# One weave delay and the writer of two constants, in a pooled-attention and mixer kernel on one core

## The chip, the core and the metric

The kernel runs on one core of one Trainium2 chip. Five engines work side by side: TensorE (PE in the profile; its weight loads are PEld), VectorE (DVE), ScalarE (ACT), GpSimd (POOL) and SyncE (SP), each with an instruction stream of its own. Transfers are issued by SyncE, GpSimd and, for one output, ScalarE. The metric is the time of one execution on the device in microseconds (us); less is better.

## What is computed

Eight batches, each with 8 heads, 576 rows and a head dimension of 64. Keys and values are averaged over groups of 8 rows, which leaves 72 of each; attention runs over these. The result, laid out as 576 x 512 per batch, goes through a mixer: one two-layer network across the rows (576 to 256 to 576) and one across the channels (512 to 1536 to 512), each with a residual.

```python
k_p = k.reshape(B, H, Sp, pool, D).mean(axis=3)
v_p = v.reshape(B, H, Sp, pool, D).mean(axis=3)
scores = scale * np.matmul(q, k_p.transpose(0, 1, 3, 2))
scores = scores - np.max(scores, axis=-1, keepdims=True)
attn = np.exp(scores)
attn = attn / (np.sum(attn, axis=-1, keepdims=True) + 1e-09)
x = np.matmul(attn, v_p)          # then laid out as (batch, 576, 512)

xt = x.transpose(0, 2, 1)
h = np.maximum(xt @ w_tok1, 0.0) @ w_tok2
u = x + h.transpose(0, 2, 1)
h2 = np.maximum(u @ w_ch1, 0.0) @ w_ch2
out = u + h2
```

## The kernel before

**Tiles.** Of a batch's 576 rows, 512 form four main blocks of 128, and 64 are a tail. The tails of two batches share one tile of 128 partitions; the groups are [0, 7], [1, 2], [3, 4], [5, 6], and a batch's slot is its place in its group. Matmul operands are bf16.

**Start.** The first batch's keys, queries and values are loaded in pieces: half of the keys as raw f32 through SyncE and cast by VectorE, the rest by GpSimd's transfers (`load_main0`, L152). Meanwhile two constant matrices are built: `pool_m` (128 x 72, L172) holds 1/8 where a row belongs to a pooled row, and `diag` (128 x 16, L180) the same for the tail, from which VectorE copies `pool_t` (L189). Each is first filled with 1/8 and then cut to a band by two affine selects on GpSimd. TensorE sums keys and values by multiplying with these matrices. `idle` is a zero tile whose matmuls keep TensorE running during the wait (L261). Instructions of this part are put in order by the framework's scheduler, per engine.

**Stages.** From `tc.manual_schedule` on, the order of the text is the order of each engine's instructions. The loop runs over b = 0 to 7. Its main stream is `c_stream(b)`, the channel network of batch b: 12 steps of hidden-layer matmuls (`do_GT`, L1007, with the ReLU L1009 on ScalarE), then for each of four row blocks three steps of output matmuls (L1023), the residual add on VectorE (L1027) and a write by SyncE (L1055). A batch in slot 1 adds the tail of its group: 3 + 3 more steps. Each step is given a cost of 864.

Beside it runs a side stream: `value_stream(b + 1)` and `score_stream(b + 2)`.

- `value_stream` begins with issues: the transpose of the next batch's queries (`qT_dma`, SyncE) and `load_gated(b + 2)` on GpSimd, which copies one element of the last transposed probabilities into `gate` (L984) and so holds back the loads behind it. Then come the steps of values: `a.do_AV` and `c.do_AV`, two of each, and `t.do_AV` for a pair of tails (cost 1150 each). One multiplies transposed probabilities `pT` with the pooled values (L468) and normalises on VectorE (L472, L473). Then `mix_stream`: the tail's part of the row network (`do_tails`, L608), the first layer for the main blocks (`do_AT`, L615, ReLU on ScalarE and VectorE), the second layer (`do_u`, L672, added on VectorE L673), and transposes of the result by SyncE's transfers (`do_uT`, L684).
- `score_stream` holds the scores (`do_S`, L390), maximum and shift on VectorE (L396, L398), the exponential on ScalarE (`do_E`, L406), and the transpose of the probabilities into `pT` by a transfer that SyncE issues (`do_PT`, L412).

**The weave.** `weave(main, side, delay, lead)` puts the two streams into one order by their costs: the main stream runs alone until `delay` of its cost is spent, and then a side item is taken whenever the side's share lies at or behind the main stream's share, with `lead` left at the end.

```python
    tm, ts = max(main.total() - delay - lead, 1e-9), max(side.total(), 1e-9)
    cm, cs = -delay, 0.0
        take_side = im >= len(main.items) or (ia < len(side.items) and cs / ts <= cm / tm)
```

A delay of 1728 is two steps of the main stream, 3456 four. The call is in the loop's last line (L1096):

```python
            weave(c_stream(b), side, 1728.0 if b == 0 else 3456.0 if b == 1 else 1728.0, 3456.0 if b == B - 2 else 1728.0)
```

Of the kernel before, what the change touches and what calls it, by code (L numbers as in the profile page):

```python
# [28 lines left out]
def weave(main, side, delay=0.0, lead=0.0):  # L29


    tm, ts = max(main.total() - delay - lead, 1e-9), max(side.total(), 1e-9)
    im = ia = 0
    cm, cs = -delay, 0.0
    while im < len(main.items) or ia < len(side.items):
        take_side = im >= len(main.items) or (ia < len(side.items) and cs / ts <= cm / tm)
        if take_side:
            c, fn = side.items[ia]
            ia += 1
            cs += c  # L40
        else:
            c, fn = main.items[im]
            im += 1
            cm += c
        fn()
# [3 lines left out]
def kernel(  # L49
# [16 lines left out]
    nc = tc.nc  # L66
    B, H, S, D = q.shape
# [4 lines left out]
    POOL = 8  # L72
# [97 lines left out]


    pool_m = singles.tile([P, SP], BF16)  # L172
    nc.gpsimd.memset(pool_m, 1.0 / POOL)
    nc.gpsimd.affine_select(out=pool_m, in_=pool_m, pattern=[[-2, SP]], compare_op=ALU.is_ge,
                            fill=0.0, base=0, channel_multiplier=1)
    nc.gpsimd.affine_select(out=pool_m, in_=pool_m, pattern=[[2, SP]], compare_op=ALU.is_ge,
# [1 line left out]

    load_main0(k, main_t[0][0], HP, H)
    diag = singles.tile([P, P // POOL], BF16)  # L180
    nc.gpsimd.memset(diag, 1.0 / POOL)
    nc.gpsimd.affine_select(out=diag, in_=diag, pattern=[[-POOL, P // POOL]], compare_op=ALU.is_ge,
                            fill=0.0, base=0, channel_multiplier=1)
    nc.gpsimd.affine_select(out=diag, in_=diag, pattern=[[POOL, P // POOL]], compare_op=ALU.is_ge,
# [747 lines left out]
    def score_stream(st, b):  # L932

        add = adder(st)
        a, c, t = parts[b]
        own = owned(b)
        add(SC, a.do_S, 0)
        add(SC, a.do_S, 1)
        add(0, a.do_E, 0)
        for bb in own[1:]:  # L940
            add(KP, pool_k, bb)
        add(SC, a.do_S, 2)
        add(0, a.do_E, 1)
        add(0, a.do_E, 2)
        add(0, a.do_PT, 0)
        add(0, a.do_PT, 1)
        if t:
            add(2 * SC, t.do_S)
        add(SC, c.do_S, 0)
        if t:  # L950
            add(0, t.do_E)
            add(0, t.do_PT)
        add(SC, c.do_S, 1)
        add(0, c.do_E, 0)
        add(SC, c.do_S, 2)
        add(0, c.do_E, 1)
        add(0, c.do_E, 2)
        add(0, c.do_PT, 0)
        add(0, c.do_PT, 1)

    def value_stream(st, b):

        add = adder(st)
        a, c, t = parts[b]
        if b + 1 < B:
            units(b + 1)
            add(0, qT_dma, b + 1)
        if b + 2 < B:
            add(0, load_gated, b + 2, lambda: c.pT[1][:, 0, 0:1])
        add(AV, a.do_AV, 0)  # L970
        add(AV, a.do_AV, 1)
        if t and len(t.bs) == 1:
            add(AV, t.do_AV)
        add(AV, c.do_AV, 0)
        if t and len(t.bs) > 1:
            add(AV, t.do_AV)
        add(AV, c.do_AV, 1)
        mix_stream(st, b, owned(b + 1)[:1] if b + 1 < B else ())
# [70 lines left out]
    def c_stream(b):  # L1049
        st = Stream()  # L1050
        g = group_of[b]

        def dst_main(j, cols, o_sb):
            q = nc.gpsimd if b == B - 2 and j == 0 else nc.sync if cols.start == 0 else nc.scalar
            q.dma_start(out=out[b, 0:MAIN, cols].rearrange("(p j) n -> p j n", j=NJ)[:, j, :], in_=o_sb)  # L1055

        def dst_tail(j, cols, o_sb):
            for s, bb in enumerate(groups[g]):
                nc.sync.dma_start(out=out[bb, MAIN:S, :], in_=o_sb[half[s], :])

        wide, chunk = channel_mix(lambda kk, t0, t1: uT_main[b][:, t0 // P:t1 // P, kk, :],
                                  lambda j: u_main[b][:, j, :], dst_main, MAIN, 0 if b else 3)
        blocks = [wide] + [chunk(j, 2 if b == B - 1 and j == NJ - 1 else 1) for j in range(NJ)]
        if slot_of[b] == 1:
            wide, chunk = channel_mix(lambda kk, t0, t1: uT_tail[g][:, kk, t0:t1], lambda j: u_tail[g], dst_tail, P)
            at = 3 if b == B - 1 else len(blocks)
            blocks[at:at] = [wide, chunk(0)]
        for block in blocks:
            st.items.extend(block)
        return st  # L1070
# [16 lines left out]
    with tc.manual_schedule(engines=engines):  # L1087
        side1 = begin()
        for b in range(B):
            side = Stream() if b else side1  # L1090
            if 0 < b < B - 1:
                value_stream(side, b + 1)
            if b + 2 < B:
                score_stream(side, b + 2)

            weave(c_stream(b), side, 1728.0 if b == 0 else 3456.0 if b == 1 else 1728.0, 3456.0 if b == B - 2 else 1728.0)  # L1096


# [28 lines left out]
```

## Time and profile before

| | |
|---|---|
| three runs | 281.32 us median, 279.86 to 281.5 |
| the profiled execution | 280.83 us, of which the span from the first to the last instruction is 279.1 |
| granted TensorE clock | 1.000 (mean) |
| TensorE busy | 268.3 us |
| VectorE, ScalarE, GpSimd busy | 165.6, 121.9, 113.4 us |
| chain that ended last, by engine | TensorE 84%, transfers 6%, VectorE 5% |
| DMA | 42.27 MB, mean 151 GB/s |

Start times are counted from the span's start. A row of the timeline gives the start, the time from the first start to the last end, the engine, the line, the operation, what it writes and reads, the shapes and how many were merged; in square brackets stands the idle time of the engine before it and what ended that. The end of a matmul is modelled: it takes in the drain, which overlaps the next matmul, so that starts are the safer thing to compare. The chain is followed back from the last instruction: at each step to what released it.

### The profile page before, as it was taken

Reading aid. Unit: us, or ns where it says so; the run is one execution under the profiler, and the core shown is the slowest. Engines: PE = TensorE matmul, PEld = TensorE weight load, DVE = VectorE, ACT = ScalarE, POOL = GpSimd, SP = SyncE. Lnnn points to the kernel's source line nnn. Section 1 sums busy time; section 2 is a strip of 40 time slices with the busy share of each in tenths; the row PEclk is TensorE's granted clock in tenths of the full one; section 3 lists DMA queues with packets and bytes.
Section 4 is the critical chain, followed back from the end, with each engine's and each line's share of the span. In section 5 each row is a group of like instructions: output and inputs, shape, how many; then the busy total and the mean of one; then the engine's idle time right before and its main releaser. Section 6 shows DMA issues by size and latency. Waiting matters only on the chain.

```text
span 279.1 us, 5476 instructions
## 1 busy us (share of the span) xinstructions
PE 268.3 (96%) x2144; PEld 145.1 (52%) x2172; DVE 165.6 (59%) x381; ACT 121.9 (44%) x225; POOL 113.4 (41%) x162
## 2 busy tenths in 40 slices
PE   6789999999999999999999999999999999999994
PEld 4565856554545444475545454475544454554462
DVE  5597677778759853684579761785479452510112
ACT  8673688235533454035534452054623550036220
POOL 8748433697538957193449264820000000000000
PEclk9999999999999999999999999999999999999999
DMA  8999999996999999959998999759266701461013
GB/s 134 176 195 205 200 205 196 190 212 140 197 153 193 222 239 153 212 151 155 173 197 144 204 199 194 162 137 162 63 84 152 180 2 39 113 100 33 38 47 105
DMA packets 98969, 42.27 MB, mean 151 GB/s; under 512 B 68800, under 2 KB 94400, under 8 KB 98944
## 3 DMA queue, kind: packets, MB, share of 16 engines
q0 software_dynamic: 35616, 17.93, 49.1%
q1 hardware_dynamic: 63184, 23.93, 42.4%
q8 instruction: 17, 0.28, 0.4%
q10 hardware_dynamic: 144, 0.07, 0.1%
q14 instruction: 8, 0.07, 0.1%
HBM read 35.85 MB, written 9.44 MB: 162 GB/s over the span
## 4 chain that ended last, share of the span: by engine, by line
PE 84%; DMA 6%; DVE 5%; issue 1%; ACT 1%; POOL 1%; DVEq 0%; POOLq 0%
PE pa L1023 31%; PE pa L1007 30%; PE pa L672 3%; DMA pT<-prob_m 3%; PE pa L390 3%; PE pa L468 3%; DMA km<-in_k_dram 2%; PE pa L597 2%; PE pa L651 1%; DVE xm L473 1%; PE pa L615 1%; PE pt L615 1%; DVE mx L396 1%; PE pa L1039 1%; PE pt L374 1%
## 5 line engine op out<-in xcount | busy, mean ns | idle before, releaser
L1023 PE MATMUL pa<-wc,GT 128*128 128x512 bf16 (+2 forms) x427 | 102.4, 373 | 1.0 <-issue 0.2
L1009 ACT ACTIVATE GT<-pa 128x512 bf16<-128x512 f32 x105 | 62.2, 597 | 64.1 <-PE pa L1007 63.8
L1007 PE MATMUL pa<-uTm,wc 128*128 128x512 bf16 x372 | 89.3, 379 | 0.0
L1007 PEld LDWEIGHTS <-wc 128*128 128x128 bf16 x564 | 44.8, 98 | 37.1 <-issue 1.6
L1023 PEld LDWEIGHTS <-GT 128*128 128x128 bf16 x444 | 40.8, 98 | 41.5 <-issue 1.2
L406 ACT ACTIVATE prob_m<-sh 128x432 bf16<-128x432 f32 (+1 forms) x48 | 24.5, 522 | 55.2 <-DVE sh L398 55.1
L1027 DVE TENSOR_TENSOR o<-pa,um 128x512 f32<-128x512 f32 (+2 forms) x33 | 22.1, 670 | 26.4 <-PE pa L1023 26.3
L357 POOL TENSOR_TENSOR s<-vs 72x512 f32<-72x512 bf16 x24 | 27.6, 1150 | 15.7 <-DMA vs<-in_v_dram 14.2
L398 DVE TENSOR_TENSOR sh<-pa,mx 128x432 f32<-128x432 f32 (+1 forms) x48 | 26.8, 558 | 4.1
L396 DVE TENSOR_REDUCE mx<-pa 128x6 f32<-128x432 f32 (+1 forms) x48 | 26.4, 550 | 4.3 <-PE pa L390 4.1
L473 DVE TENSOR_TENSOR xm<-pa,den 128x256 bf16<-128x256 f32 x56 | 23.7, 424 | 1.9
L1055 POOL DMA_DIRECT2D out_dram<-o x1 | 0.6, 620 | 49.1 <-DVE o L1027 49.1
L472 DVE RECIPROCAL den<-pa 128x4 f32<-128x4 f32 x60 | 10.6, 176 | 16.8 <-PE pa L468 16.7
L673 DVE TENSOR_TENSOR um<-pa,xm 128x512 bf16<-128x512 f32 x24 | 16.1, 687 | 5.0 <-PE pa L672 3.7
L358 POOL TENSOR_TENSOR s<-s 72x256 f32<-72x256 f32 x24 | 17.3, 722 | 1.9
L390 PE MATMUL pa<-kbd,qT 128*128 128x144 bf16 x128 | 15.2, 226 | 0.9 <-ACT qT L378 0.7
L390 PEld LDWEIGHTS <-qT 128*128 128x128 bf16 x128 | 10.6, 98 | 9.3 <-ACT qT L378 1.3
L468 PEld LDWEIGHTS <-pT 72*128 72x128 bf16 (+1 forms) x256 | 11.2, 99 | 8.1 <-DMA pT<-prob_m 1.4
L593 DVE TENSOR_SCALAR AT<-pa 128x512 bf16<-128x512 f32 x6 | 4.1, 692 | 16.9 <-PE pa L615 9.5
L672 PE MATMUL pa<-AT,w2m 128*128 128x512 bf16 x45 | 13.1, 379 | 0.0
L468 PE MATMUL pa<-vpx,pT 72*128 72x65 bf16 (+1 forms) x256 | 12.6, 194 | 0.5 <-DMA pT<-prob_m 0.4
L1007 PE MATMUL pa<-uTt,wc 128*128 128x128 bf16 x192 | 11.9, 219 | 0.0
(151 smaller groups left out, 273.5 us busy)
## 6 DMA issues: line engine op xcount, KB each, us to landing
out_dram<-o SPq DMA_DIRECT2D x30, 256.0 KB, 2.6
vs<-in_v_dram POOLq DMA_DIRECT2D x7, 512.0 KB, 10.7
km<-in_k_dram POOLq DMA_DIRECT2D x7, 512.0 KB, 9.6
qm<-in_q_dram POOLq DMA_DIRECT2D x7, 512.0 KB, 12.8
wc<-in_moe_w_ch_dram POOLq DMA_DIRECT2D x6, 512.0 KB, 11.7
out_dram<-o SPq DMA_DIRECT2D x8, 128.0 KB, 2.4
o<-in_k_dram SPq DMA_DIRECT2D x2, 256.0 KB, 3.0
kt<-in_k_dram POOLq DMA_DIRECT2D x8, 64.0 KB, 8.0
```

The lines of the kernel that those rows point to most:

```text
L357: nc.gpsimd.tensor_tensor(out=s4, in0=vs[:, hs, 0:4], in1=vs[:, hs, 4:8], op=add)
L390: nc.tensor.matmul(out=sc[:, (h - h0) * 2:(h - h0) * 2 + 2, :], lhsT=qTs[self.b][:, 2 * h + self.jj, :], rhs=kbd[self.b % NB][:, h], start ...
L396: nc.vector.tensor_reduce(out=mx[:, 0:n], in_=sc, axis=AX.X, op=ALU.max)
L398: nc.vector.tensor_tensor(out=sh[:, 0:n], in0=sc, in1=mx[:, 0:n, None].broadcast_to([P, n, SP]), op=ALU.subtract)
L406: nc.scalar.activation(out=self.probs[:, :, h0:h1, 0:SP].rearrange("p e h n -> p h e n"), in_=self.sh[i][:, 0:(h1 - h0) * 2].rearrange("p ...
L468: nc.tensor.matmul(out=ao[r, hh, :], lhsT=probs_of(h, r), rhs=vpx[b % NB][:, h, :], start=True, stop=True)
L473: nc.vector.tensor_tensor(out=xo[rows, hf * HP * D:(hf + 1) * HP * D].rearrange("p (h d) -> p h d", d=D), in0=ao[rows, :, 0:D], in1=den[ro ...
L672: nc.tensor.matmul(out=u_ps, lhsT=w2m[:, m, j, :], rhs=ATs[b][:, m, :], start=(m == 0), stop=(m == 1))
L1007: nc.tensor.matmul(out=g_ps[:, i, :], lhsT=wc1[:, kk, m * P:(m + 1) * P], rhs=uTs(kk, 0, width), start=(kk == 0), stop=(kk == 3))
L1009: nc.scalar.activation(out=GT[:, m0:m0 + per, :], in_=g_ps, func=AF.Relu)
L1023: nc.tensor.matmul(out=hold["ps"], lhsT=GT[:, kk, j * P:(j + 1) * P], rhs=wc2[:, kk, cols], start=(kk == 0), stop=(kk == NM - 1))
L1027: nc.vector.tensor_tensor(out=o_sb, in0=hold["ps"], in1=us(j)[:, cols], op=ALU.add)
```

## The change

In the weave of b == 2 the main stream runs four steps alone and not two, before the side stream (the values of batch 3, which is the fourth batch, and the scores of batch 4) sets in; the lead at the end stays. And the fills of `pool_m` and `diag` with 1/8 are issued on VectorE and not on GpSimd; the affine selects that follow remain on GpSimd.

```diff
     pool_m = singles.tile([P, SP], BF16)
-    nc.gpsimd.memset(pool_m, 1.0 / POOL)
+    nc.vector.memset(pool_m, 1.0 / POOL)
     nc.gpsimd.affine_select(out=pool_m, in_=pool_m, pattern=[[-2, SP]], compare_op=ALU.is_ge,
                             fill=0.0, base=0, channel_multiplier=1)
...
     diag = singles.tile([P, P // POOL], BF16)
-    nc.gpsimd.memset(diag, 1.0 / POOL)
+    nc.vector.memset(diag, 1.0 / POOL)
...
-            weave(c_stream(b), side, 1728.0 if b == 0 else 3456.0 if b == 1 else 1728.0, 3456.0 if b == B - 2 else 1728.0)
+            weave(c_stream(b), side, 1728.0 if b == 0 else 3456.0 if b <= 2 else 1728.0, 3456.0 if b == B - 2 else 1728.0)
```

## The prediction, made before the change was run

> **What bounds the kernel now.** I read the page's busy times first, then the windows of 10 us, then the chain of waits with TensorE's timeline around the stage that the change touches, and at last the start.
>
> ```profile
> PE 268.3 (96%) x2144; PEld 145.1 (52%) x2172; DVE 165.6 (59%) x381; ACT 121.9 (44%) x225; POOL 113.4 (41%) x162
> ```
>
> Three lines of the windows follow (stretch, its length, busy us of PE, weight loads, DVE, ACT, POOL, then the granted clock, DMA share, GB/s):
>
> ```profile
> 0.00:10.00 10.00, 6.95 (x71) 4.74 (x72) 4.70 (x18) 7.74 (x17) 8.78 (x22) 1.00 0.99 146
> ...
> 30.00:40.00 10.00, 10.00 (x92) 7.03 (x91) 7.47 (x15) 7.86 (x16) 3.09 (x5) 1.00 1.35 202
> ...
> 90.00:100.00 10.00, 9.59 (x64) 4.75 (x64) 8.02 (x19) 5.05 (x10) 8.78 (x12) 1.00 1.23 221
> ```
>
> TensorE (PE) is the bound. From 30 us to the end most windows show it idle for 0.05 of 10 us; the worst is 90 to 100, with 0.41. Little is to be won after the start: what moves TensorE's stream by x moves the end by x, unless a later wait takes it.
>
> The changed delay acts on the third batch's channel stage (b == 2), which begins at 94.94 us. Here is TensorE there, and below it the stage of b == 4, which has the same make (a second slot, a delay of 1728, the values of a batch that opens a group, the scores of one that closes it):
>
> ```profile
> 94.94 1.89 PE L1007 MATMUL pa<-uTm,wc 128*128 128x512 bf16 x8
> 97.19 0.43 PE L468 MATMUL pa<-vpx,pT 72*128 72x65 bf16 x8 [0.36 <-DMA pT<-prob_m]
> 99.19 0.42 PE L468 MATMUL pa<-vpx,pT 72*128 72x65 bf16 x8
> 101.44 0.43 PE L468 MATMUL pa<-vpx,pT 72*128 72x65 bf16 x8
> ...
> 156.80 1.89 PE L1007 MATMUL pa<-uTm,wc 128*128 128x512 bf16 x8
> 158.53 0.42 PE L468 MATMUL pa<-vpx,pT 72*128 72x65 bf16 x8
> 160.51 0.42 PE L468 MATMUL pa<-vpx,pT 72*128 72x65 bf16 x8
> 162.50 0.42 PE L468 MATMUL pa<-vpx,pT 72*128 72x65 bf16 x8
> ```
>
> In both, two blocks of hidden-layer matmuls (L1007) run, then a step of values (L468), then two blocks, and so on. Undisturbed, the steps stand at +1.73, +3.71 and +5.70 us from the stage's start; with b == 2 at +2.25, +4.25 and +6.50. So the first step is late by 0.52 (2.25 - 1.73) and the third by a further 0.27 (6.50 - 4.25 = 2.25, against 1.99). Only 0.36 of it is listed as idle, because the drain that is modelled at a matmul's end covers the rest. The whole stage agrees: 94.94 to 128.37 is 33.43 us, 156.80 to 189.42 is 32.62; the difference is 0.81. The chain of waits names what both steps waited for:
>
> ```profile
> 91.01 6.13 DMA pT<-prob_m
> 97.19 0.43 PE pa L468 x8
> 97.63 0.56 PE pa L1007 x3
> 98.18 3.21 DMA pT<-prob_m
> 101.44 0.43 PE pa L468 x8
> ```
>
> These are transposes of probabilities by DMA, issued by SyncE. The first lands 6.13 us after its issue, the others from 98 us on in 3.2 to 3.3.
>
> **The change part by part.** *The delay.* I worked the weave through by its costs (main 25920, side 17198). Before, the side begins after two blocks of 864, now after four; `lead` is as it was, so it ends at the same place. The first step of values moves from 94.94 + 1.73 (where it can't start) to 94.94 + 3.45 = 98.39, as the stage of b == 1 shows it with the same delay (x16 of L1007 in 3.45 us). Its transpose has landed at 97.15. The second follows at 98.39 + 1.99 = 100.38; its transpose was there before 99.19. The third comes at 102.37; its transpose landed at 101.39. The last two move by as much, and their transposes are in by 102.78. So both waits go: 0.52 + 0.27 = 0.79 us, with 0.80 as the mean of this and the 0.81 of the whole stage.
>
> What is late next? The side is denser (20736 of main work for it and not 22464), and some steps change neighbours. Between the second token matmuls (AT1) and their first reader (u0) one block is left and not two: the ReLU on VectorE takes 0.69 us and starts 0.04 after TensorE's end, so the operand is there after about 0.75, and the matmul that reads it comes after 0.86 + 0.22 = 1.08. Hidden, with 0.3 to spare; if VectorE were still at the output add before it (0.69, one block earlier, so just done) the price is 0.1 to 0.3. The first token matmuls come 2.5 us after the last step of values begins (step 0.27, two blocks, four tail matmuls 0.5), and its rows were ready after 1.5 us (104.79 to 106.30). The stage of b == 1, which packs 21640 of side work into 15552, loses about 0.4 us in 20 with that, and this one packs 17198 into 20736: I take 0, between 0 and 0.3.
>
> SyncE's queue: the transpose of q of batch 4 is issued with the side's first step, but stands behind the same issues as before. Then the first `uT` transpose comes after the second output write (one issue of 0.33 us) and not before it; the next stage reads it 8 us later. GpSimd's queue: the gate copy, the loads of batch 5 and their sums keep their order, and the gate still opens when the fourth transpose lands (102.78).
>
> The scores of batch 4 fall one block later within the stage, except at its end. Their first transpose is issued at 123.95 now, right after the last output write. With TensorE 0.8 earlier, VectorE's row of shifts (0.61, 0.46 each) and adds (0.69) puts that write's add at 122.25 to 122.94, and so the transpose at about 123.4. It took 4.7 us there, so it lands near 128.1; its reader comes at 130.09 - 0.80 = 129.29. 1.2 us to spare: cost 0.
>
> *The two constants.* GpSimd loses memsets of 0.177 and 0.102 us. VectorE gains two. A 128x36 memset takes 0.088 there and a 64x256 one 0.27; 72 elements stand near 0.12, 16 near 0.07, together 0.19. They lie before VectorE's wait for the raw keys (idle 0.77 before 3.63), so they cost nothing; without that cover, 0.19. The warm-up matmuls wait for a VectorE memset there: late by up to 0.19, they push the first half of the keys' sums from 8.19, but the second half waits for the keys until 9.54, with TensorE idle 0.87 before it.
>
> New is a wait of the first mask (affine select) on GpSimd for VectorE; behind it are queued the key load and all further loads. VectorE is done by about 2.4, before GpSimd has issued the load ahead (2.97).
>
> ```profile
> 2.18 0.79 POOL L153 DMA_DIRECT2D qm<-in_q_dram  x1
> 2.97 0.18 POOL L173 MEMSET pool_m<- 128x72 bf16 x1
> 3.06 0.75 POOL L153 DMA_DIRECT2D km<-in_k_dram  x1
> 3.89 0.27 POOL L174 TENSOR_SCALAR_AFFINE_SELECT pool_m<-pool_m 128x72 bf16<-128x72 bf16 x1
> ```
>
> The key load that the start waits for (it lands at 9.5) is issued right behind the memset. Without it the issue can come 0.09 to 0.18 earlier; but the order here is a scheduler's, not the text's, and a mask that needs no memset on its own engine may now be put ahead of it: both masks (0.27 + 0.24) less the memset make it 0.33 later. Bounds: -0.18 and +0.33. I take 0, because the load ahead landed 5.3 us after its issue and this one after 6.4: 1.1 us of it are queueing, and an issue that moves by less changes only the time in the queue.
>
> The GPSIMD Engine Reference of the Trainium skill (section 4.1) says to use VectorE for elementwise work, GpSimd being at best near line rate for one input. By that alone the 0.28 us would count as a gain and the sum would be 279.75; the queueing above speaks against it.
>
> Sum: 280.83 us for the profiled execution (span 279.1, 1.73 around it) less 0.80 is 280.03. The three runs have a median of 281.32 and scatter from 279.86 to 281.5; the mean of these and the profiled one is 280.88, and 0.80 less is **280.1**, which I forecast.
>
> **The rivals.** *The wait moves one batch on* (slower than before). In the stage of b == 3 the first step of values reads the first transpose of batch 4. If that is issued a block later than now (124.81, because its shift is), and lands as slowly as the 6.13 of batch 3, it is there at 130.94, against 129.29: 1.65 lost, 0.80 won, 281.7. It decides against the change from a landing after 130.09 on. For it: the 4.7 now, so it is not a quiet place. Against it: the write ahead of it in SyncE's queue comes earlier, not later. The slow one fell among heavy traffic (221 to 250 GB/s at 90 to 97 us); at 121 to 124 us the rows show 87 GB/s, and batch 5's values had landed at 118.18. DMA: Bandwidth & Descriptors of the Trainium skill (Queues, rings and completion order) says that a DMA engine takes turns between queues packet by packet, so loads in flight would stretch a transpose; no row shows the turns themselves. 8%.
>
> *A later wait takes the gain.* Loads gated by time alone don't come earlier: 280.9. Against it: the keys of batch 6 are paired at 143.27 and read at 147.42, the values of batch 5 summed at 128.35 and read at 158.53, so 4 us and more are left. 14%.
>
> *The start moves.* The queueing doesn't cover the key load's issue: 279.8 to 280.4. 10%.
>
> *Only the listed idle is a real wait:* 0.36 won, 280.5. Against it is the 0.81 of the twin stage. 8%.
>
> **How the numbers follow.** My forecast has 54%, the four rivals 40%, and 6% are for what no row shows, above all an order at the start that holds up other loads. The range takes the forecast with 0.9 below it for scatter (half of the 1.64 of the three runs) and reaches up to the slower rival: 279.2 to 281.7. A measurement of this kernel tells about 1% (2.8 us) from no change. Faster than 278.1 would need more than all of TensorE's idle time between 30 and 270 us (2.0 us, summed over the windows): 2%. Slower than 283.7 comes from the unnamed 6% and the tail of the slower rival: 6%. The rest, 92%, lies between.
>
> **What would show it.** The changed profile should show L1007 x16 in one piece before the first L468 of the stage, no idle before it, steps of values 1.99 apart, a stage of 32.6 us, and less of "DMA pT" in the chain (3.3% now; two pieces of it gone). The key load at the start should land at 9.4 to 9.6 wherever its issue stands. I am wrong if L468 of the stage of b == 3 shows a wait for pT, if the stage stays above 33 us, or if TensorE's work of that stage starts more than 0.3 us away from 94.94.

## The result and the profile after

The changed kernel takes 279.69 us in the median of 14 runs (279.27 to 280.48), the kernel before 280.98 in 14 runs (279.61 to 282.25). The ratio is 0.9951 with a 95% interval of 0.9934 to 0.9968, that is 1.38 us less (0.90 to 1.85): a small gain of half a percent, clear of the scatter. The runs also lie closer together, 1.2 us from the lowest to the highest and not 2.6. The profiled execution takes 279.91 us, with a span of 277.8. So the time is 0.92 us less than that of the profile before and the span 1.3 less: what lies outside the span has grown, by some 0.4 us.

TensorE's timeline of the changed kernel, in the third batch's stage and at the beginning of the next:

```profile
94.79 3.62 PE L1007 MATMUL pa<-uTm,wc 128*128 128x512 bf16 x16
98.24 0.42 PE L468 MATMUL pa<-vpx,pT 72*128 72x65 bf16 x8
100.23 0.42 PE L468 MATMUL pa<-vpx,pT 72*128 72x65 bf16 x8
102.22 0.42 PE L468 MATMUL pa<-vpx,pT 72*128 72x65 bf16 x8
...
127.41 1.89 PE L1007 MATMUL pa<-uTm,wc 128*128 128x512 bf16 x8
129.13 0.42 PE L468 MATMUL pa<-vpx,pT 72*128 72x65 bf16 x8
```

Four hidden-layer steps stand in one piece (x16), no step of values has idle time in brackets, and the steps follow each other by 1.99 us. The stage runs from 94.79 to 127.41, 32.62 us, against 33.43 before and 32.62 in its twin at b == 4. The window in which TensorE idled most answers to that, and so does the page's chain by engine, in which the transfers fall from 6% to 2%:

```profile
90.00:100.00 10.00, 9.95 (x59) 4.93 (x59) 7.41 (x17) 5.30 (x11) 8.56 (x12) 1.00 1.23 223
```

```profile
PE 89%; DVE 4%; DMA 2%; ACT 1%; issue 1%; POOL 1%; DVEq 0%; POOLq 0%
```

At the start, the changed kernel's timeline of GpSimd has no fill between the two loads, but the order behind them is another one too:

```profile
2.18 0.79 POOL L153 DMA_DIRECT2D qm<-in_q_dram  x1
2.97 0.75 POOL L153 DMA_DIRECT2D km<-in_k_dram  x1
3.71 0.23 POOL masks.py:197 MEMSET ident<- 128x128 bf16 x1
3.85 0.76 POOL L153 DMA_DIRECT2D qm<-in_q_dram  x1
4.68 0.28 POOL L174 TENSOR_SCALAR_AFFINE_SELECT pool_m<-pool_m 128x72 bf16<-128x72 bf16 x1
```

The scheduler put the second half of the queries 0.79 us earlier (3.85, it was 4.64) and the first mask that much later. The stages begin 0.15 to 0.17 us earlier in this profile (34.39 for 34.56, 64.99 for 65.15, 94.79 for 94.94), before the changed delay can act. So TensorE's last row ends 1.02 us earlier, at 274.26 and not 275.28: about 0.15 from the start, 0.81 from the stage, and 0.06 from the stage of b == 6. Whether the 0.15 belongs to the constants, and why the runs show more than 0.81, the profile of one execution can't say.

### The profile page after: what moved, and what is told of

Read it like the earlier page. It is cut to its first block, busy times and chain, and to the rows that moved or that the text cites. A ratio compares the mean times of both kernels' runs of the same rounds, so it can differ in the third digit from the quotient of the medians.

```text
span 277.8 us, 5476 instructions
## 1 busy us (share of the span) xinstructions
PE 267.6 (96%) x2144; PEld 145.2 (52%) x2172; DVE 166.0 (60%) x383; ACT 121.8 (44%) x225; POOL 113.3 (41%) x160
## 4 chain that ended last, share of the span: by engine, by line
PE 89%; DVE 4%; DMA 2%; ACT 1%; issue 1%; POOL 1%; DVEq 0%; POOLq 0%
PE pa L1023 33%; PE pa L1007 31%; PE pa L672 3%; PE pa L390 3%; PE pa L468 3%; DMA km<-in_k_dram 2%; PE pa L597 2%; PE pa L651 1%; PE pa L615 1%; DVE xm L473 1%; PE pt L615 1%; PE pa L1039 1%; PE pt L374 1%; PE pa L677 1%; PE pa L635 1%
## 5 line engine op out<-in xcount | busy, mean ns | idle before, releaser
L269 POOL COPY kk<-km 128x1024 bf16<-128x1024 bf16 x8 | 8.1, 1037 | 10.8 <-DMA km<-in_k_dram 10.8
```

## The experiments

Each kernel below was timed beside the kernel before, in runs that alternated on one chip. Two theories stand against each other: that the delay carries the gain by taking TensorE out of a wait for transposes whose landing varies, and that the constants at the start carry a part of it.

**The delay alone.**

```diff
-            weave(c_stream(b), side, 1728.0 if b == 0 else 3456.0 if b == 1 else 1728.0, ...
+            weave(c_stream(b), side, 1728.0 if b == 0 else 3456.0 if b <= 2 else 1728.0, ...
```

> The kernel before with the delay of 3456 at b == 2; the constants stay on GpSimd. If the delay carries the whole gain (my theory): the third batch's stage lasts 32.6 us and not 33.4, its first step of values has no wait, TensorE's work of that stage starts at 94.9 as before, and the median is 0.8 to 1.4 us below the kernel before (ratio 0.995 to 0.997), with runs as close together as those of the changed kernel. If the constants carry a part, it falls short of the changed kernel's 0.9951 by that part: 0.15 us if the start of the two profiles tells it, 0.5 us if the whole remainder over 0.8 is theirs.

Measured: 279.72 us (279.43 to 280.42), ratio 0.9958 (0.9938 to 0.9977). The stage lasts 32.62 us. That is all of the gain that can be told apart, and the narrower scatter came with it.

**The constants alone.**

```diff
-    nc.gpsimd.memset(pool_m, 1.0 / POOL)
+    nc.vector.memset(pool_m, 1.0 / POOL)
...
-    nc.gpsimd.memset(diag, 1.0 / POOL)
+    nc.vector.memset(diag, 1.0 / POOL)
```

> The kernel before with both fills on VectorE; the delay stays 1728. My prediction: the start is bound by the queue of loads, so the key load lands at 9.3 to 9.5 us, the third batch's stage lasts 33.4 us, and the time is that of the kernel before within 0.2 us. If the start counts: key load 0.1 to 0.2 us earlier, all stages after it by the same, 0.15 to 0.5 us less in the median.

Measured: 281.58 us, ratio 1.0012 (0.9986 to 1.0038): no gain that can be told, and by the interval none above 0.4 us. What shows in every run is another thing: the time outside the span is 2.10 to 2.17 us in the 12 runs of this kernel and 1.65 to 1.77 in those of the kernel before beside them. It is 2.10 to 2.22 in every run of the other kernels with the new constants, and 1.65 to 1.77 in every run with the old ones but those of the kernel with earlier loads below, which has 1.84 to 1.95. So moving the fills adds some 0.43 us that no view of the span shows. Its cause stays open, and so does whether the span gives it back; the ratio of 1.0012 fits both.

Its profile tells more about the delay than about the constants, since the wait has grown:

```profile
94.66 1.89 PE L1007 MATMUL pa<-uTm,wc 128*128 128x512 bf16 x8
97.84 0.43 PE L468 MATMUL pa<-vpx,pT 72*128 72x65 bf16 x8 [1.29 <-DMA pT<-prob_m]
99.84 0.42 PE L468 MATMUL pa<-vpx,pT 72*128 72x65 bf16 x8
102.22 0.43 PE L468 MATMUL pa<-vpx,pT 72*128 72x65 bf16 x8 [0.23 <-DMA pT<-prob_m]
```

Nothing that the constants do lies near this place, yet the first step stands 3.18 us into the stage (2.25 in the first profile), and the stage lasts 34.49 us.

**The kernel before, profiled once more.**

> The kernel before, unchanged, for a second profile. If the wait for the transposes is the same in each execution: stage 33.4 us, wait 0.36 listed. If it varies, as the wider scatter of the runs before (2.6 us against 1.2 after) suggests: a stage that differs from 33.4 by more than 0.2 us, while all other stages keep their length within 0.1. The start of the stages should again be near 94.94; if it is nearer to 94.8, the 0.15 us between the two profiles is scatter and not the constants.

Measured: 281.34 us, ratio 1.0011 (0.9988 to 1.0033). TensorE's timeline:

```profile
94.40 1.89 PE L1007 MATMUL pa<-uTm,wc 128*128 128x512 bf16 x8
96.90 0.43 PE L468 MATMUL pa<-vpx,pT 72*128 72x65 bf16 x8 [0.61 <-POOL vpx L359]
```

The stage lasts 33.72 us; the others keep their lengths within 0.1. The bracket names GpSimd's sums, but the ones that end at 96.86 are those of batch 4, by their order in the kernel's text; the sums of batch 3, which this step reads, were done at 89.15. The transpose that it reads was issued at 90.47 and landed 6.4 us later, at about 96.9. The two events stand close together, and the profile put the wait down to the wrong one. The stage begins 0.54 us earlier than in the first profile of the same program, so the 0.15 us between the profiles of before and after is within the scatter of the start.

**Three steps alone, and six.**

```diff
-            weave(c_stream(b), side, 1728.0 if b == 0 else 3456.0 if b == 1 else 1728.0, ...
+            weave(c_stream(b), side, 1728.0 if b == 0 else 3456.0 if b == 1 else 2592.0 if b == 2 else 1728.0, ...
```

> The kernel before with a delay of 2592 at b == 2 (three steps alone and not two or four); constants on GpSimd. From the profile before, the first step of values would stand 2.59 us into the stage, its transpose landed at 2.21; the third at 6.57, its transpose at 6.45: both waits gone by a small margin, the gain that of four steps, 0.8 us. If landings vary by half a us from run to run, three steps don't always cover them: a gain between 0.4 and 0.8, and a wider scatter than with four.

Measured: 280.38 us (279.51 to 281.26), ratio 0.9972 (0.9949 to 0.9994). The margin of 0.4 us that one profile promised wasn't there in this one:

```profile
94.76 2.75 PE L1007 MATMUL pa<-uTm,wc 128*128 128x512 bf16 x12
97.91 0.43 PE L468 MATMUL pa<-vpx,pT 72*128 72x65 bf16 x8 [0.39 <-DMA pT<-prob_m]
```

The transpose landed 7.00 us after its issue at 90.86. With six (`5184.0 if b == 2`):

> The kernel before with a delay of 5184 at b == 2: six steps alone. If four already cover every landing: stage 32.6 us, median as with four (279.7), scatter the same. If four leave a wait in some executions: a little less, up to 0.2 us, and a narrower scatter. If the denser side costs something: a stage above 32.7 us.

Measured: 279.73 us (279.05 to 280.66), ratio 0.9944 (0.9926 to 0.9962), stage 32.62 us. Two more steps neither gain nor cost anything that can be told; the denser side is free.

**The backlog taken away, with the old delay.** Why does this transpose take 6 to 7 us where others take 3.3? Batch 4's loads and three quarters of batch 3's values, 2 MB in all, are issued together from 73 us on; that is the backlog. The last of them, the queries, is issued at 76.45 and lands 16.5 us later, at about 92.95, and the transposes of batch 2's result, issued at 82 to 84 us, take about 10. This kernel loads batch 3's values earlier:

```diff
-        add(0, load_v, 3, 0, 2)
+        add(0, load_v, 3, 0, H)
...
         if b == 4:
-            load_v(3, 2, H)
+            pass
```

> The kernel before (delay 1728, constants on GpSimd), but the values of batch 3 are loaded in one piece in the first stage and not to three quarters behind the gate of batch 4's loads; the same bytes in all. If the wait comes from a backlog of loads that holds the transposes up (loads of batch 4 land until 93 us, transposes issued at 84 land 10 us later): 432 KB less in that backlog brings the transposes of batch 2's result and batch 3's first probabilities 1 to 2.5 us earlier, the first one in 3.2 to 5 us after its issue and not in 6 to 7, and the third batch's stage lasts 32.6 to 32.9 us with the old delay. If it is the order in the weave alone that matters (the step simply stands too early after its exponentials), the landing stays at 6 to 7 us and the stage at 33.4 or more. The bytes come earlier into a busy stretch; a stage of b == 0 longer than 30.6 would show what that costs.

Measured: 280.52 us (279.73 to 281.45), ratio 0.9972 (0.9945 to 0.9998). TensorE in the third batch's stage, with the old delay of two steps:

```profile
95.89 1.89 PE L1007 MATMUL pa<-uTm,wc 128*128 128x512 bf16 x8
97.61 0.42 PE L468 MATMUL pa<-vpx,pT 72*128 72x65 bf16 x8
99.60 0.42 PE L468 MATMUL pa<-vpx,pT 72*128 72x65 bf16 x8
101.59 0.42 PE L468 MATMUL pa<-vpx,pT 72*128 72x65 bf16 x8
```

No wait, and a stage of 32.62 us. The first transpose, issued at 91.96, has this row in the view of transfers (the last figure is the time to landing):

```profile
pT<-prob_m SPq DMA_TRANSPOSE x1, 3.3
```

SyncE's queue shows more. First two rows of the kernel before, then the same issues of this one (start, time of the issues, x the number):

```profile
91.01 5.05 SPq L412 DMA_TRANSPOSE pT<-prob_m  x2
96.16 0.53 SPq L1055 DMA_DIRECT2D out_dram<-o  x1
```

```profile
91.96 2.67 SPq L412 DMA_TRANSPOSE pT<-prob_m  x2
95.13 0.33 SPq L1055 DMA_DIRECT2D out_dram<-o  x1
```

With the backlog, even issuing two transposes holds SyncE for 5.05 us, without it for 2.67, and the first lands after 3.3 us and not 6.1. This also explains the wait of the third step: its transpose stands behind them in SyncE's queue and is issued 3.24 us into the stage, here 1.87. But in this profile 0.88 us of the gain is given back two stages earlier. There the loads that were moved meet those of the weights, and the stage of b == 1 begins late:

```profile
66.09 1.24 PE L1007 MATMUL pa<-uTm,wc 128*128 128x512 bf16 x5 [0.65 <-DMA uTm<-um]
```

That transpose was issued at 59.16 and landed 6.79 us later, where the kernel before shows 3.6: the same kind of backlog at another place, the stage before it 31.48 us long and not 30.6. A wait taken away at its cause came back where the cause went. How much of it comes back in other executions is not shown: by the ratio the runs are 0.79 us faster than the kernel before (0.06 to 1.55), more than the 1.13 of the table below less 0.88 would leave.

On this, the page DMA: Bandwidth & Descriptors of the Trainium skill (Queues, rings and completion order) says that a DMA engine takes turns between the queues packet by packet. The 6.1 us of the transpose with the loads in flight and the 3.3 without them agree with that; the turns themselves no run here shows.

**A later issue at the start.**

```diff
+    [nc.gpsimd.memset(singles.tile([P, SP], BF16, name=f"late{i}"), 0.5) for i in range(4)]
     nc.gpsimd.memset(pool_m, 1.0 / POOL)
```

> The kernel before with four more fills of 72 columns on GpSimd (into tiles that nothing reads) between the query load and the key load at the start: the key load is issued some 0.4 to 0.7 us later than 3.06. Queue theory (my prediction): it still lands at 9.4 to 9.6 and the key sums of the second half start there. If the issue decides: landing and start later by as much, 9.9 to 10.2, and with them every stage.

Measured: 281.72 us, ratio 1.0020 (0.9991 to 1.0048). GpSimd's and TensorE's rows of the start:

```profile
2.97 0.45 POOL L173 MEMSET late<- 128x72 bf16 x4
3.34 0.18 POOL L173 MEMSET pool_m<- 128x72 bf16 x1
3.43 0.87 POOL L153 DMA_DIRECT2D km<-in_k_dram  x1
...
9.04 0.44 PE L308 MATMUL pa<-pool_m,km 128*64 128x64 bf16 x16 [0.38 <-DMA km<-in_k_dram]
```

The key load is issued 0.37 us later, and yet the sums that wait for it begin at 9.04, earlier than the 9.54 of the first profile. With the old constants and no added fills, five further profiles have them at 8.68 to 9.34; with the new ones, five have 9.14 to 9.37. A shift of the issue by some tenths is lost in a scatter of 0.9.

**One more step of the same kind, on top of the change.** The profile before shows another wait, at b == 1: the token matmuls follow right behind the last step of values, whose rows VectorE has still to normalise. The key sums of batch 3 can stand between them.

```diff
+        early = pooled if b == 2 else ()
+        for bb in early:
+            add(KP, pool_k, bb)
         add(864 if g > 1 else 1080, do_AT, 0)
         add(864 if g > 1 else 1080, do_AT, 1)
-        for bb in pooled:
+        for bb in pooled if b != 2 else ():
             add(KP, pool_k, bb)
```

> The changed kernel, and at b == 1 the sums of batch 3's keys are woven ahead of the token matmuls and not behind them. TensorE loses 0.3 to 0.5 us there (b == 1: the third of four token matmuls starts 0.97 after the first, against 0.43, and waits for VectorE's normalised rows). If the sums fill this gap: the stage of b == 1 lasts 29.3 to 29.5 us and not 29.8, the median is 279.3. If the wait only moves on (the ReLU for the second layer, now closer to it): stage 29.8.

Measured: 279.46 us (279.15 to 280.22), ratio 0.9932 (0.9906 to 0.9958); the stage of b == 1 lasts 29.49 us. TensorE before, with the gap between 74.20 and 75.17 (two matmuls take 0.43), and in this kernel, where four run in one piece:

```profile
74.20 0.81 PE L597 MATMUL pa<-xm,w1m 128*128 128x512 bf16 x2
75.17 0.38 PE L597 MATMUL pa<-xm,w1m 128*128 128x512 bf16 x1
```

```profile
75.26 1.03 PE L597 MATMUL pa<-xm,w1m 128*128 128x512 bf16 x4
```

It was run again beside the changed kernel:

> The changed kernel with batch 3's key sums woven ahead of the token matmuls at b == 1, beside the changed kernel itself. The stage of b == 1 was 29.49 and not 29.80: if that reaches the end, the median lies 0.3 us below the changed kernel's; if a later wait takes it, the two are equal within 0.1.

> The changed kernel again, on the same chip as the next one. The third batch's stage should last 32.6 us whatever the landing of its transposes (5.9 to 7.2 so far), and the stages should start anywhere between 94.4 and 95.3; median 279.6 to 279.8.

Measured: 279.56 us (279.08 to 280.09), ratio 0.9937 (0.9918 to 0.9956), against 280.06 (279.67 to 280.60) and 0.9954 (0.9937 to 0.9971) for the changed kernel. The stage of b == 1 shows 29.49 again. The two intervals overlap, but both are taken against a third kernel. Set against each other, the 6 and 7 runs differ by 0.55 us in the mean (95% interval 0.1 to 1.0), and the stage's 0.31 us is there in both profiles. Its medians are the lowest of this study.

The second profile of the changed kernel has its own lesson. The third batch's stage lasts 32.62 us, but it begins late:

```profile
95.30 3.61 PE L1007 MATMUL pa<-uTm,wc 128*128 128x512 bf16 x16 [0.43 <-DVE sh L398]
```

The stage of b == 1 before it lasts 30.40 us, 0.60 more than in the other profiles with the same order of steps. VectorE's row is named, but in the first profile before the same row ended at 95.39, after the stage had begun at 94.94. What fits is the stage's own operand: the second transpose of batch 2's result was issued at 83.96 and landed 11.3 us later, at about 95.3; in the first profile before it was there by 93.7. So it seems that the backlog can hit a second reader, which the change doesn't protect.

All profiles of the third batch's stage (us; the landing is the issue plus the time that the profile gives for it):

```
kernel         delay  stage from  pT issued  lands after  at     first step  stage lasts
before         1728   94.94       91.01      6.1          97.1   97.19       33.43
before_again   1728   94.40       90.47      6.4          96.9   96.90       33.72
const_only     1728   94.66       90.77      7.0          97.8   97.84       34.49
late_issue     1728   94.78       90.93      5.9          96.8   96.84       33.35
delay_three    2592   94.76       90.86      7.0          97.9   97.91       33.50
after          3456   94.79       90.86      6.2          97.1   98.24       32.62
after_again    3456   95.30       91.30      7.0          98.3   98.75       32.62
delay_only     3456   95.30       91.37      6.3          97.7   98.75       32.62
pool_first     3456   94.26       90.33      5.9          96.2   97.71       32.62
pool_first_2   3456   94.34       90.41      5.3          95.7   97.80       32.62
delay_six      5184   94.64       90.80      7.2          98.0   99.82       32.62
v3_early       1728   95.89       91.96      3.3          95.3   97.61       32.62
```

Where the first step stands right behind the landing, the stage lasts 0.7 to 1.9 us longer; where it doesn't, the stage has one length to the hundredth. With four steps the room is 0.4 us at the least among these profiles (98.3 and 98.75); the landing of delay_six, at 98.0, would have left four steps 0.1. The four profiles with the delay of 1728 and the backlog (the first four rows) lose 1.13 us in the mean (33.75 - 32.62).

## Why the prediction was right, and where its size was off

**The delay.** The mechanism is shown: the delay alone gives the gain, and taking the backlog away removes the same wait with the delay untouched. The term of the sum was too small. It put 0.80 us, from one execution, as if the wait had one size. The runs show 1.38 for the change (0.90 to 1.85) and 1.58 for six steps (1.07 to 2.08); the 1.18 for the delay alone (0.65 to 1.74, from its ratio and 280.94 before) would still hold 0.80. The profiles show waits of 0.73 to 1.87 with a mean of 1.13. The comparison with the twin stage was a good ruler for that one execution (0.81 by the twin, 0.81 won between the two profiles); it says nothing of the next.

**What would be late next.** The denser side cost nothing, as taken: 32.62 us is the twin's length. The one block between the second token matmuls and their reader is enough: VectorE's add ends at 111.67, the ReLU runs from 111.84 to 112.53, and the pair of matmuls of which the second needs it begins at 112.50 without a wait. The next stage's first transpose is issued at 123.20 (predicted 123.4), takes 4.0 us (4.7 were assumed), and its reader comes at 129.13 (129.29).

**The constants.** Zero was right within what the runs can tell, but not as reasoned. The sum carried over the 1.73 us outside the span, and with the new constants they are 2.11 in the profiled execution; that this doesn't show in the medians was not foreseen and stays unexplained. VectorE's fills take 0.12 and 0.07 us as estimated. The masks did not go ahead of the key load; what moved ahead was the second half of the queries, which the prediction hadn't thought of, and neither mattered. The rule of the GPSIMD Engine Reference of the Trainium skill (section 4.1), to keep elementwise work off GpSimd, is not what the time shows here: the fills are shorter on VectorE, and the 0.28 us that GpSimd saves are not seen at the end (ratio 1.0012). That the load's issue is hidden by a queue was argued: the later issue agrees with it, but the scatter of the start is larger than the shift.

**The rivals.** That the wait moves one batch on: not in any profile of the changed kernel. That a later wait takes the gain: the stages after the third keep their lengths within 0.1 us, so it passes to the end. That the start moves: the start does move, by up to 0.9 us, but from run to run and not with the constants. That only the listed idle of 0.36 counts: 0.81 came back, so the idle that a row lists is not the whole of a wait here.

**The criteria.** A stage start of more than 0.3 us off 94.94 was to show an error. It was a bad test: the kernel before itself gives 94.40 in its second profile. The key load was to land at 9.4 to 9.6, and that was too narrow too: the sums that wait for it begin at 8.68 to 9.54 in the twelve profiles. And the runs, 14 of each kernel, tell half a percent from no change, where the prediction took 1%.

What stays open is why the same transposes take 5.3 to 7.2 us from one execution to the next with the same loads in flight, and how often the stage's own operand is late as in the second profile of the changed kernel.

## What to carry to other kernels

A wait on a transfer in one profile is a sample. Before a step is moved by just the margin that this profile asks for, look at how long the transfer takes in other executions, or leave a step more: three would have covered the first profile and failed in another, four and six held in all six profiles that have them, at no cost that can be told, since another part of the work could run there. A neighbouring stage of the same make, with no wait in it, is a better ruler for what a wait costs than the idle time in brackets. And loads that aren't urgent can delay small transfers that are. Here moving the reader was cheap, while moving the loads took a part of the backlog elsewhere.

## What the hardware showed that was not expected

Under load it isn't only the landing that stretches. The issue of one of the first two probability transposes holds SyncE's queue for 2.0 to 3.2 us (1.3 without the backlog), and the later issues of that engine stand behind it. A transpose issued some 8 us after the last of the 2 MB of loads, with the queries still in flight, landed up to 11.3 us later. And the third batch's stage, where no wait is in it, lasts 32.62 us in each of seven profiles, while its beginning lies anywhere from 94.26 to 95.89. Apart from what an edit moved, the stages up to there differ in length by more than 0.1 us only where TensorE stood waiting: for the probabilities' transpose in this stage, for a transpose of the result at b == 0 in the kernel with the earlier loads, and, as argued above, once at b == 1.
